# Leaving PSUM by wide ScalarE copies and normalising on GpSimd, in a top-k attention and PReLU kernel

## The chip, the cores and the metric

The kernel runs on one core of a Trainium2 chip. The time is that of one whole execution on the device, in microseconds (us). The core has engines that run side by side, each in the order of its own instruction stream: TensorE (PE; its weight loads are PEld), VectorE (DVE), ScalarE (ACT), GpSimd (POOL) and SyncE (SP), which here only starts transfers. They meet through semaphores: an instruction that needs a result waits, and everything behind it on the same engine waits too.

## The reference

Eight batches of eight heads, 576 rows of width 64. Each row of scores keeps only its 32 largest entries before the softmax; the attention output, laid out as 4608 tokens by 512, goes through two matrix products with a PReLU between them.

```python
scores = scale * np.matmul(q, k.transpose(0, 1, 3, 2))
kth = np.partition(scores, -32, axis=-1)[..., -32:-31]
scores = np.where(scores >= kth, scores, -1e9)
attn = np.exp(scores - scores.max(-1, keepdims=True))
attn = attn / (attn.sum(-1, keepdims=True) + 1e-9)
x = np.matmul(attn, v)            # then tokens x 512
h = x @ w_in
out = (np.maximum(h, 0) + alpha * np.minimum(h, 0)) @ w_out
```

## The kernel before, in words

Work goes by pairs of heads (32 pairs, four to a batch). The rows of a pair make nine row tiles of 128 x 576 scores, so there are 288 row tiles, numbered n. The program is written out by hand in **ticks**, one row tile per tick: a loop over n emits for each engine what it does in that tick, and small tables (`put`, `run`) hold work for a later tick of a given engine. Nothing reorders it afterwards.

One row tile passes the engines like this:

- PE makes the scores into PSUM (`scores`, L335). ACT copies them out with a pivot added (`act_b`, L344, tile `b`), counts how many lie on one side of the pivot (`act_s`, L349, `h`, with an accumulator read) and takes the exponential of two tiles at once (`act_e`, L354, `e`).
- POOL turns the count into a sign (`side_of`, L359, `SG`) and flips the scores by it (`flip`, L365, `y`; two buffers). In tick n it flips tile n-1.
- DVE takes the eight largest of each of five segments of `y` (L376, tile n-2 in tick n), merges those lists (L390, L392, tile n-3), and applies the resulting limit to the exponentials (`weights`, L443, tile n-7, the first DVE instruction of a tick). In one tick of three it compares counts (`sel_eq`, L408, `EQ`). For that POOL has prepared `ra` in two steps: `sel_a` (L398) in the tick before and `sel_a2` (L403) right behind the flip in the same tick. `limit` (L424, `KP`) is POOL's too.
- The weights go to a transposing transfer started by SP (L457). When those of a half pair are there, PE multiplies them with v (`av`, L495) into a PSUM tile `pu`, four or six blocks of 65 columns: 64 products and a sum of the weights. DVE takes the reciprocal of the sums (`av_rz`, tile `rz`), and `av_out` (L524, ACT) writes product times reciprocal into the row buffers `xb` (128 rows) and `xm` (64 rows), one instruction per head and chunk. SP transposes `xb` into `xT` for the two matrix products (`x_turn`, L569), whose steps fill PE and ACT between the ticks.

A pair is cut in two halves. With j the tick modulo 9, the first half (g = 0: four blocks) has `av` in a tick with j = 4, the second (g = 1: six blocks, two of them 64 rows) in one with j = 1. Pairs 0 to 26 leave PSUM through `av_out`; pair 27 does it on DVE (`dve_out`), the last batch through `out_last`, also on DVE. Neither is touched.

Of the kernel before, what the change touches and what calls it, by code (L numbers as in the profile page):

```python
# [9 lines left out]
FP32 = mybir.dt.float32  # L10
BF16 = mybir.dt.bfloat16
I32 = mybir.dt.int32
AF = mybir.ActivationFunctionType
ALU = mybir.AluOpType
# [17 lines left out]
def kernel(  # L32
# [10 lines left out]
    nc = tc.nc  # L43
    B, H, S_, D = q.shape
    NTOK, DM = out.shape
# [5 lines left out]
    KPB = H // 2  # L51
# [39 lines left out]
    prep = main.enter_context(tc.tile_pool(name="prep", bufs=2))  # L91
    attn = main.enter_context(tc.tile_pool(name="attn", bufs=4))
# [36 lines left out]
    pairs = {}  # L129
# [32 lines left out]
    n = 0  # L162
    while n < NT:
        m = 1 if ORDER[n][1] == 8 and ORDER[n + 1][1] != 8 else 2
# [291 lines left out]
            d["wT", j // 2] = wT  # L456
            nc.sync.dma_start_transpose(wT, d["w2"])  # L457

    xb, xm = {}, {}

    def check_group(g):
        nc.vector.tensor_reduce(out=M8[:, g * TPP:g * TPP + TPP], in_=Cs.pop(g)[:, :, :, 7],
# [24 lines left out]

    def x_tiles(b):
        if b not in xb:
            xb[b] = [prep.tile([128, DM], BF16, name="xb", bufs=6) for _ in range(4)]  # L490
            xm[b] = prep.tile([64, DM], BF16, name="xm", bufs=1)

    def av_one(o_, d, wT, side, cs):
# [4 lines left out]
    def av(p, g):  # L498
        d = pairs[p]
        x_tiles(p // KPB)  # L500
        d["pu", g] = pu = ps_d.tile([128, 4 + 2 * g, V1], FP32, name="pu", tag="pd")
        for i in range(2):
            for side in range(2):
                av_one(pu[:, 2 * i + side, :], d, d["wT", 2 * g + i], side, slice(0, 128))
        if g == 1:
            for side in range(2):
                av_one(pu[0:64, 4 + side, :], d, d["wTm"], side, slice(64 * side, 64 * side + 64))

    def av_rz(p, g):
        d = pairs[p]  # L510
        d["rz", g] = rz = attn.tile([128, 6], FP32, name="rz", bufs=4)
        nc.vector.reciprocal(rz[:, 0:4], d["pu", g][:, 0:4, D])
        if g == 1:
            nc.vector.reciprocal(rz[0:64, 4:6], d["pu", g][0:64, 4:6, D])

    def av_out(p, g):
        d = pairs[p]
        b, kt = p // KPB, p % KPB
        pu, rz = d["pu", g], d["rz", g]
        for c in range(4 + 2 * g):  # L520
            m = 128 if c < 4 else 64
            h0 = 128 * kt + 64 * (c % 2)
            dst = xb[b][2 * g + c // 2][:, h0:h0 + 64] if c < 4 else xm[b][:, h0:h0 + 64]
            nc.scalar.activation(dst, pu[0:m, c, 0:D], AF.Copy, scale=rz[0:m, c:c + 1])  # L524

    def dve_out(p, g):
        d = pairs[p]
        b, cs = p // KPB, slice(128 * (p % KPB), 128 * (p % KPB) + 128)
        pu, rz = d["pu", g], d["rz", g]
        for c in range(0, 4 + 2 * g, 2):  # L530
            m = 128 if c < 4 else 64
            dst = xb[b][2 * g + c // 2] if c < 4 else xm[b]
            nc.vector.tensor_tensor(
                dst[:, cs].rearrange("p (s d) -> p s d", s=2), pu[0:m, c:c + 2, 0:D],
                rz[0:m, c:c + 2].unsqueeze(2).to_broadcast([m, 2, D]), ALU.mult)
# [3 lines left out]
    def av_last(i, g):  # L539
        x_tiles(B - 1)  # L540
        m = 128 if i < 4 else 64
        pul[i, g] = pu = ps_d.tile([128, 4, V1], FP32, name="pu", tag="pd")
        for s in range(2):
            d = pairs[P0 + 2 * g + s]
            for side in range(2):
                cs = slice(0, 128) if i < 4 else slice(64 * side, 64 * side + 64)
                av_one(pu[0:m, 2 * s + side, :], d, d["wT", i] if i < 4 else d["wTm"], side, cs)

    def rz_last(i, g):
        m = 128 if i < 4 else 64  # L550
        rz = attn.tile([128, 6], FP32, name="rz", bufs=4)
        nc.vector.reciprocal(rz[0:m, 0:4], pul[i, g][0:m, :, D])
        pul[i, g] = pul[i, g], rz

    def out_last(i, g):
        m = 128 if i < 4 else 64
        pu, rz = pul.pop((i, g))
        dst = xb[B - 1][i] if i < 4 else xm[B - 1]
        nc.vector.tensor_tensor(
            dst[:, 256 * g:256 * g + 256].rearrange("p (s d) -> p s d", s=4), pu[0:m, :, 0:D],  # L560
            rz[0:m, 0:4].unsqueeze(2).to_broadcast([m, 4, D]), ALU.mult)

    def x_turn(b, chunks):
        for i in chunks:
            c0 = (b * S + 128 * i) % NX
            if b == B - 1:
                c0 = b * S % NX + (64 + 128 * i if i < 4 else 0)
            if i < 4:
                nc.sync.dma_start_transpose(xT[:, :, c0:c0 + 128], xb[b][i])  # L569
            else:  # L570
                nc.sync.dma_start_transpose(xT[:, :, c0:c0 + 64], xm[b])
# [4 lines left out]
    def turn_last(h):  # L576
        pool, tag = (ps_a, "pa") if h == 0 else (ps_m, "misc")
        xa = pool.tile([128, 2, 128], BF16, name="xa", tag=tag)
        for j in range(2):
            c0 = 128 * (2 * h + j)  # L580
            nc.tensor.transpose(xa[:, j, :], xb[B - 1][3][:, c0:c0 + 128], ident_b)
        nc.vector.tensor_copy(xT[:, 2 * h:2 * h + 2, CL:CL + 128], xa)
# [205 lines left out]
    with tc.manual_schedule(engines={E.PE, E.Activation, E.DVE, E.Pool, E.SP}):  # L788
        cal = {}

        def put(tick, eng, f):
            cal.setdefault((tick, eng), []).append(f)
# [11 lines left out]
        def feed(lim):  # L804
            while blocks and blocks[0][0] + blocks[0][1] <= lim:
                back.extend(mlp_steps(*blocks.pop(0)))
# [12 lines left out]
        def tail_of(n, wn):  # L819
            wp, wj = ORDER[wn]  # L820
            b = wp // KPB
            if wp < P0:
                if wj == 3:
                    put(n + 3, "pe", lambda: av(wp, 0))
                    put(n + 4, "dve", lambda: av_rz(wp, 0))
                    if wp == P0 - 1:
                        put(n + 4, "dvx", lambda: dve_out(wp, 0))
                    else:
                        put(n + 6, "act", lambda: av_out(wp, 0))
                    if wp % KPB == KPB - 1 and b >= 5:  # L830
                        dt = 4 if wp == P0 - 1 else 6
                        put(n + dt, "end", lambda: x_turn(b, (0, 1)))
                        put(n + dt + 2, "end", lambda: feed(b * S + 256))
                if wj == 8:
                    put(n + 4, "pe", lambda: av(wp, 1))
                    put(n + 5, "dve", lambda: av_rz(wp, 1))
                    if wp == P0 - 1:
                        put(n + 5, "dvx", lambda: dve_out(wp, 1))
                    else:
                        put(n + 7, "act", lambda: av_out(wp, 1))  # L840
                    if wp % KPB == KPB - 1:
                        dt = 5 if wp == P0 - 1 else 7
                        put(n + dt, "end", lambda: x_turn(b, range(2 if b >= 5 else 0, 5)))
                        put(n + dt + 2, "end", lambda: feed((b + 1) * S))
            elif (wj == 8 or wj % 2) and wp % 2:
                i, g = wj // 2, (wp - P0) // 2
                dt = 2
                if i == 3 and g == 1:
                    put(n + dt, "pe", flush)
                put(n + dt, "pe", lambda: av_last(i, g))  # L850
                where = "end" if i == 3 and g == 0 else "dvx"
                put(n + dt + 1, where if where == "end" else "dve", lambda: rz_last(i, g))
                put(n + dt + 1, where, lambda: out_last(i, g))
                if i == 3:
                    if g == 1:
                        put(n + dt + 1, where, lambda: last_ph(0))
                    put(n + dt + 2 - g, where, lambda: turn_last(g))
                    if g == 1:
                        put(n + dt + 1, where, lambda: (last_ph(1), last_pz()))
                elif g == 1:  # L860
                    put(n + dt + 1, "dvx", lambda: x_turn(b, (i,)))
                    put(n + dt + 2, "end", lambda: back.extend(mlp_steps(*last.pop(i))))
# [23 lines left out]
        n = 0  # L886
        end = max(NT + 24, 0)
        while n < end or back or after:
# [20 lines left out]
            if n < NT:  # L909
                n0, m, i = unit_of[n]  # L910
# [82 lines left out]
            for wn in due:  # L993
                turn(wn)
                tail_of(n, wn)
# [152 lines left out]
```

## Time and profile before

| | |
|---|---|
| three runs | 817.95, 819.47, 822.98 us (median 819.47) |
| the profiled execution | 820.06 us, of which 818.2 us span from first to last instruction |
| busy, share of the span | DVE 95%, ACT 92%, PE 86%, POOL 73% |
| mean granted TensorE clock | 0.947 of full speed |

A busy share is a mean over the whole span; how far an engine is filled in one stretch is read from the view by stretches. In the rows below, times are microseconds from the start of the span unless marked ns; what stands in brackets behind an instruction is the idle time of its engine just before it and what ended that.

### The profile page before, as it was taken

How to read it: one execution, taken by the hardware profiler on the slowest of the kernel's cores; microseconds unless marked ns; L12 is line 12 of the kernel's file. 1: busy time of each engine (PE TensorE's matmuls, PEld its weight loads, DVE VectorE, ACT ScalarE, POOL GpSimd, SP SyncE). 2: the span in 40 equal slices, each digit the busy share in tenths (PEclk: the TensorE clock that was granted, in tenths of full speed). 3: DMA queues.
4: the chain of work that ended last, by engine and by line, in shares of the span. 5: the costliest groups of instructions: out<-in, count | busy, mean ns of one | idle time of the engine just before them, and what ended most of it. 6: DMA issues, size and time to landing. Idle time of an engine off the chain costs nothing. (4 is left out here: it accounts for less than half of the span.)

```text
span 818.2 us, 20527 instructions
## 1 busy us (share of the span) xinstructions
PE 701.8 (86%) x5705; PEld 419.7 (51%) x5780; DVE 774.3 (95%) x4464; ACT 750.8 (92%) x1730; POOL 594.9 (73%) x1052
## 2 busy tenths in 40 slices
PE   7876779878978799888988789978898989999977
PEld 4533445444545446444544345644455565665755
DVE  5999999999999999999999999999999999999973
ACT  6998999999999999999999999999999999988842
POOL 5787777777777878777687777776777867676630
PEclk8587779899999999999999999999999999999999
DMA  7899985656666565565577546664556653455332
GB/s 150 170 165 174 166 141 107 122 111 97 145 140 135 98 133 122 116 123 103 124 162 123 111 97 138 121 140 96 107 127 132 121 116 87 94 108 100 84 77 59
DMA packets 343001, 99.06 MB, mean 121 GB/s; under 512 B 335056, under 2 KB 335328, under 8 KB 342880
## 3 DMA queue, kind: packets, MB, share of 16 engines
q1 hardware_dynamic: 337808, 94.73, 58.5%
q0 software_dynamic: 3584, 2.39, 2.6%
q8 instruction: 47, 0.77, 0.4%
q10 hardware_dynamic: 1488, 0.56, 0.3%
q14 instruction: 74, 0.61, 0.2%
HBM read 36.71 MB, written 9.44 MB: 56 GB/s over the span
## 5 line engine op out<-in xcount | busy, mean ns | idle before, releaser
L365 POOL TENSOR_TENSOR y<-SG,b 128x576 int32<-128x576 int32 x288 | 417.2, 1449 | 97.3 <-DVE C L376 86.7
L376 DVE MAX8 C<-y 128x8 f32<-128x112 f32 (+1 forms) x1440 | 384.0, 267 | 3.8 <-POOL y L365 3.8
L335 PE MATMUL ps<-qkT 64*128 64x288 f32 (+1 forms) x1280 | 243.8, 457 | 17.1 <-ACT b L344 16.7
L344 ACT ACTIVATE b<-ps,T 128x576 f32<-128x576 f32 x288 | 206.6, 759 | 13.6 <-PE ps L335 13.6
L443 DVE SCALAR_TENSOR_TENSOR w<-b,KP,e 128x576 bf16<-128x576 f32 x256 | 204.5, 800 | 2.3 <-POOL KP L424 2.2
L349 ACT ACTIVATE h<-b 128x576 bf16<-128x576 f32 x288 | 201.8, 701 | 2.5
L735 PE MATMUL ph<-xT,w_in_b 128*128 128x128 bf16 (+2 forms) x997 | 143.2, 285 | 50.9 <-ACT gT L741 40.4
L354 ACT ACTIVATE e<-b 128x1152 bf16<-128x1152 f32 (+1 forms) x158 | 173.7, 1099 | 0.0
L335 PEld LDWEIGHTS ps<-qkT 64*128 64x128 f32 (+1 forms) x1280 | 127.8, 187 | 79.7 <-ACT b L344 39.1
L390 DVE MAX8 L<-C 128x8 f32<-128x40 f32 x864 | 160.4, 186 | 0.2
L359 POOL TENSOR_SCALAR SG<-S_all 128x1 int32<-128x1 f32 x288 | 82.4, 286 | 96.2 <-ACT h L349 72.2
L735 PEld LDWEIGHTS <-w_in_b 128*128 128x128 bf16 x1024 | 80.2, 99 | 105.0 <-issue 80.2
L753 PE MATMUL pz<-w_out_b,gT 128*128 128x512 bf16 x544 | 132.3, 380 | 1.2 <-issue 0.3
L392 DVE MATCH_REPLACE8 C<-L,C 128x40 f32<-128x40 f32 x576 | 105.5, 183 | 0.0
L741 ACT ACTIVATE gT<-ph 128x512 bf16<-128x512 f32 x140 | 85.7, 619 | 15.2 <-PE ph L735 14.7
L753 PEld LDWEIGHTS <-gT 128*128 128x128 bf16 x560 | 51.7, 98 | 69.7 <-issue 13.2
L495 PE MATMUL pu<-v_bf,wT 128*128 128x65 bf16 (+1 forms) x1600 | 69.1, 198 | 10.4 <-DMA wT<-w 8.8
L495 PEld LDWEIGHTS <-wT 128*128 128x128 bf16 (+1 forms) x1600 | 65.1, 103 | 20.9 <-DMA wT<-w 9.3
L349 ACT ACTIVATION_READ_ACCUMULATOR h<-b 128x1 f32 x288 | 61.7, 214 | 0.0
L524 ACT ACTIVATE xb<-pu,rz 128x64 bf16<-128x64 f32 x216 | 51.9, 356 | 0.0
L392 DVE MATCH_VALUE_LOAD C<-L,C 128x8 f32 x576 | 41.6, 72 | 0.1
L758 ACT COPY o_sb<-pz 128x512 f32<-128x512 f32 x35 | 20.5, 587 | 17.8 <-PE pz L753 17.8
(117 smaller groups left out, 715.9 us busy)
## 6 DMA issues: line engine op xcount, KB each, us to landing
out_dram<-o_sb SPq DMA_DIRECT2D x34, 256.0 KB, 2.3
st_q<-in_q_dram SPq DMA_DIRECT2D x64, 128.0 KB, 2.8
kst<-in_k_dram SPq DMA_DIRECT2D x62, 128.0 KB, 2.6
st_v<-in_v_dram SPq DMA_DIRECT2D x60, 128.0 KB, 2.7
w_stage<-in_moe_w_out_dram SPq DMA_DIRECT2D x16, 256.0 KB, 4.0
w_in_b<-in_moe_w_in_dram POOLq DMA_DIRECT2D x8, 256.0 KB, 6.5
wT<-w SPq DMA_TRANSPOSE x128, 3.3
st_q<-in_q_dram SPq DMA_DIRECT2D x32, 32.0 KB, 2.6
```

The source lines that it names most:

```text
L335: nc.tensor.matmul(o_, l_, r_, start=True, stop=True)
L344: nc.scalar.activation(t["b"].rearrange("p (a c) -> p a c", a=2), t["ps"], AF.Identity, bias=T0[:, p * TPP + j:p * TPP + j + 1], scale=-ON ...
L349: nc.scalar.activation(h, tiles[n]["b"], AF.Sign, accum_out=S_all[:, n:n + 1])
L354: nc.scalar.activation(e, tiles[n0]["bu"], AF.Exp, scale=-scl)
L365: nc.gpsimd.tensor_tensor(t["y"].bitcast(I32), SG[:, n:n + 1].to_broadcast([128, S]), t["b"].bitcast(I32), ALU.subtract)
L376: return [lambda g=g: nc.vector.max(out=C[:, n % TPP, g, :], in_=y[:, g:S // 8:NSEG, :]) for g in range(NSEG)]
L390: ops.append(lambda r=r, src=src: nc.vector.max(out=L[:, 8 * r:8 * r + 8], in_=src))
L392: ops.append(lambda r=r, src=src: nc.vector.match_replace(out=C2, in_to_replace=L[:, 8 * r:8 * r + 8], in_values=src, imm_value=NEG))
L443: nc.vector.scalar_tensor_tensor(out=w_dst(n), in0=t["b"], scalar=row_limit(n), in1=t["e"], op0=ALU.is_le, op1=ALU.mult)
L495: nc.tensor.matmul(o_, wT[:, 4 * side + c, cs], d["v"][:, 5 * side + c, :], start=(c == 0), stop=(c == 4))
L735: nc.tensor.matmul(hold[f][:, i, :], w_in_b[:, kk, (f + i) * 128:(f + i + 1) * 128], xT[:, kk, c0:c0 + tb], start=(kk == 0), stop=(kk == N ...
L753: nc.tensor.matmul(pz[0:m], hold["gT"][:, f, r0:r0 + m], w_out_b[:, f, :], start=False, stop=(f == NFT - 1))
```

## The change

`av_out` is replaced by two steps. `av_copy` (ACT) copies the products out of PSUM without scaling: one instruction of 128 x 256 into a new float32 tile `ou` (one buffer), and for the second half one more of 64 x 128. `av_norm` (POOL) multiplies `ou` by the broadcast reciprocals `rz` into the row buffers, one instruction for both chunks of 128 rows, and one more for the 64 rows. For that, two chunks share one `xb` tile of 128 x 2 x 512; there are three such tiles instead of six of half the size. The ACT step stands two ticks earlier than before (at +4 and +5 in place of +6 and +7), the POOL step one tick behind it. Pair 27 and the last batch keep their DVE steps.

```diff
     def x_tiles(b):
         if b not in xb:
-            xb[b] = [prep.tile([128, DM], BF16, name="xb", bufs=6) for _ in range(4)]
+            xbt[b] = [prep.tile([128, 2, DM], BF16, name="xb", bufs=3) for _ in range(2)]
+            xb[b] = [xbt[b][i // 2][:, i % 2, :] for i in range(4)]
             xm[b] = prep.tile([64, DM], BF16, name="xm", bufs=1)
...
-    def av_out(p, g):
+    def av_copy(p, g):
         d = pairs[p]
-        b, kt = p // KPB, p % KPB
-        pu, rz = d["pu", g], d["rz", g]
-        for c in range(4 + 2 * g):
-            m = 128 if c < 4 else 64
-            h0 = 128 * kt + 64 * (c % 2)
-            dst = xb[b][2 * g + c // 2][:, h0:h0 + 64] if c < 4 else xm[b][:, h0:h0 + 64]
-            nc.scalar.activation(dst, pu[0:m, c, 0:D], AF.Copy, scale=rz[0:m, c:c + 1])
+        d["ou"] = ou = attn.tile([128, 6, D], FP32, name="ou", bufs=1)
+        nc.scalar.copy(ou[:, 0:4, :], d["pu", g][:, 0:4, 0:D])
+        if g == 1:
+            nc.scalar.copy(ou[0:64, 4:6, :], d["pu", g][0:64, 4:6, 0:D])
+
+    def av_norm(p, g):
+        d = pairs[p]
+        b, cs = p // KPB, slice(128 * (p % KPB), 128 * (p % KPB) + 128)
+        ou, rz = d["ou"], d["rz", g]
+        nc.gpsimd.tensor_tensor(
+            xbt[b][g][:, :, cs].rearrange("p c (s d) -> p c s d", s=2),
+            ou[:, 0:4, :].rearrange("p (c s) d -> p c s d", s=2),
+            rz[:, 0:4].rearrange("p (c s) -> p c s", s=2).unsqueeze(3).to_broadcast([128, 2, 2, D]),
+            ALU.mult)
+        if g == 1:
+            nc.gpsimd.tensor_tensor(
+                xm[b][:, cs].rearrange("p (s d) -> p s d", s=2), ou[0:64, 4:6, :],
+                rz[0:64, 4:6].unsqueeze(2).to_broadcast([64, 2, D]), ALU.mult)
...
-                        put(n + 6, "act", lambda: av_out(wp, 0))
+                        put(n + 4, "act", lambda: av_copy(wp, 0))
+                        put(n + 5, "pool", lambda: av_norm(wp, 0))
...
-                        put(n + 7, "act", lambda: av_out(wp, 1))
+                        put(n + 5, "act", lambda: av_copy(wp, 1))
+                        put(n + 6, "pool", lambda: av_norm(wp, 1))
```

Where the new instructions land on POOL, in the middle of the program. `L359` is `SG`, `L365` the flip; `L398`, `L403` make `ra`, `L424` makes `KP`, `L203` converts v. POOL before, two ticks with j = 3 and j = 6 and what lies between:

```order
L365 TENSOR_TENSOR y<-SG,b_6517 128x576
L398 TENSOR_SCALAR ra<-S_all 128x3
L424 TENSOR_TENSOR KP<-SG,KK 128x3
L359 TENSOR_SCALAR SG<-S_all 128x1
L365 TENSOR_TENSOR y<-SG,b_6517 128x576
L403 TENSOR_TENSOR ra<-ra 128x3
L359 TENSOR_SCALAR SG<-S_all 128x1
L365 TENSOR_TENSOR y<-SG,b_6607 128x576
L203 CAST v_bf_119<-st_v_113 128x4x64
```

POOL with the change, the same place:

```order
L365 TENSOR_TENSOR y<-SG,b_6484 128x576
L398 TENSOR_SCALAR ra<-S_all 128x3
L424 TENSOR_TENSOR KP<-SG,KK 128x3
L528 TENSOR_TENSOR xb<-ou,rz 128x2x128
L534 TENSOR_TENSOR xm<-ou,rz 64x128
L359 TENSOR_SCALAR SG<-S_all 128x1
L365 TENSOR_TENSOR y<-SG,b_6484 128x576
L403 TENSOR_TENSOR ra<-ra 128x3
L359 TENSOR_SCALAR SG<-S_all 128x1
L365 TENSOR_TENSOR y<-SG,b_6579 128x576
```

The second half's two multiplications stand between `KP` and `SG`: ahead of the sign, of the flip that needs it, and of the `ra` that follows that flip. The first half's place, three ticks on (j = 6), before:

```order
L398 TENSOR_SCALAR ra<-S_all 128x3
L424 TENSOR_TENSOR KP<-SG,KK 128x3
L451 COPY wm<-wm 128x64
L359 TENSOR_SCALAR SG<-S_all 128x1
L365 TENSOR_TENSOR y<-SG,b_6720 128x576
```

and with the change:

```order
L398 TENSOR_SCALAR ra<-S_all 128x3
L424 TENSOR_TENSOR KP<-SG,KK 128x3
L451 COPY wm<-wm 128x64
L528 TENSOR_TENSOR xb<-ou,rz 128x2x128
L359 TENSOR_SCALAR SG<-S_all 128x1
L365 TENSOR_TENSOR y<-SG,b_6688 128x576
L403 TENSOR_TENSOR ra<-ra 128x3
```

Here one multiplication has come in at the same spot, again ahead of sign, flip and `ra`. The instructions of DVE and their order are the same before and with the change.

## Rows read from the trace of the kernel before

**Rows 1.** The page: busy us, share of the span, instructions.

```profile
PE 701.8 (86%) x5705; PEld 419.7 (51%) x5780; DVE 774.3 (95%) x4464; ACT 750.8 (92%) x1730; POOL 594.9 (73%) x1052
```

**Rows 2.** By stretches: length, busy per engine with count, clock, DMA share, GB/s.

```profile
45.00:130.00 85.00, 61.20 (x419) 36.16 (x425) 82.16 (x481) 80.45 (x185) 65.30 (x115) 0.78 0.93 157
130.00:690.00 560.00, 488.35 (x3922) 282.17 (x3980) 553.43 (x3202) 540.31 (x1284) 432.08 (x754) 0.98 0.60 120
690.00:818.00 128.00, 115.66 (x1169) 80.12 (x1177) 105.01 (x574) 92.21 (x181) 66.56 (x115) 0.98 0.42 88
```

**Rows 3.** What DVE waited for from 45 to 690: total us, times, longest.

```profile
DVE P L244 <- PE pr L238: 2.3, 4, 0.8
DVE EQ L408 <- POOL ra L403: 2.1, 4, 0.7
DVE w L443 <- POOL KP L424: 0.8, 1, 0.8
DVE rz L512 <- PE pu L495: 0.6, 1, 0.6
```

**Rows 4.** Timeline of POOL around a tick with j = 3: start, us, instruction.

```profile
356.37 0.19 POOL L424 TENSOR_TENSOR KP<-SG,KK 128x3 int32<-128x3 int32 x1
356.53 0.23 POOL L359 TENSOR_SCALAR SG<-S_all 128x1 int32<-128x1 f32 x1
357.02 1.57 POOL L365 TENSOR_TENSOR y<-SG,b 128x576 int32<-128x576 int32 x1 [0.27 <-DVE C L376]
358.56 0.19 POOL L403 TENSOR_TENSOR ra<-ra 128x3 f32<-128x3 f32 x1
```

**Rows 5.** Timeline of DVE, the same stretch.

```profile
356.79 0.80 DVE L443 SCALAR_TENSOR_TENSOR w<-b,KP,e 128x576 bf16<-128x576 f32 x1
...
359.03 0.15 DVE L273 TENSOR_TENSOR sq<-M,sq 128x9 f32<-128x9 f32 x1
359.09 0.22 DVE L408 TENSOR_TENSOR EQ<-ra,iota 128x72 f32<-128x72 f32 x1
...
359.42 0.80 DVE L443 SCALAR_TENSOR_TENSOR w<-b,KP,e 128x576 bf16<-128x576 f32 x1
```

**Rows 6.** Timeline of POOL around a tick with j = 6, and DVE's two rows there.

```profile
364.15 0.23 POOL L451 COPY wm<-wm 128x64 bf16<-128x64 bf16 x1
365.54 0.23 POOL L359 TENSOR_SCALAR SG<-S_all 128x1 int32<-128x1 f32 x1 [1.16 <-DVE w L443]
365.86 1.14 POOL L365 TENSOR_TENSOR y<-SG,b 128x576 int32<-128x576 int32 x1
...
364.66 0.81 DVE L443 SCALAR_TENSOR_TENSOR w<-b,KP,e 128x576 bf16<-128x576 f32 x1
...
367.18 0.23 DVE L408 TENSOR_TENSOR EQ<-ra,iota 128x72 f32<-128x72 f32 x1 [0.25 <-POOL ra L403]
```

**Rows 7.** One line each: count, ns min/median/max of the flip and of `SG`.

```profile
L365 POOL TENSOR_TENSOR y<-SG,b x288: 1143/1571/1577, 12.4 to 788.7; 128x576 int32<-128x576 int32 x144
L359 POOL TENSOR_SCALAR SG<-S_all x288: 207/226/892, 12.0 to 788.4; 128x1 int32<-128x1 f32 x144
```

**Rows 8.** Groups by shape: busy us, mean ns of one, idle before and its releasers.

```profile
L203 POOL CAST v_bf<-st_v 128x192 bf16<-128x192 f32 x60 | 20.3, 340 | 0.0
L424 POOL TENSOR_TENSOR KP<-SG,KK 128x3 int32<-128x3 int32 x96 | 18.4, 192 | 7.7 <-DVE KK L418 7.7
L203 POOL CAST v_bf<-st_v 128x256 bf16<-128x256 f32 x30 | 11.9, 397 | 0.0
L220 ACT COPY qkT<-pt 128x128 f32<-128x128 f32 x32 | 8.3, 260 | 0.0
L618 ACT COPY o_sb<-pz 128x256 f32<-128x256 f32 x2 | 0.7, 372 | 2.8 <-SPq L1013 1.8 <-PE pz L615 1.0
L408 DVE TENSOR_TENSOR EQ<-ra,iota 128x72 f32<-128x72 f32 x96 | 21.6, 225 | 7.2 <-POOL ra L403 4.9
```

**Rows 9.** Timeline of ACT: the steps out of PSUM, second and first half.

```profile
309.36 0.94 ACT L524 ACTIVATE xb<-pu,rz 128x64 bf16<-128x64 f32 x4
310.15 0.52 ACT L524 ACTIVATE xm<-pu,rz 64x64 bf16<-64x64 f32 x2
...
317.90 0.93 ACT L524 ACTIVATE xb<-pu,rz 128x64 bf16<-128x64 f32 x4
```

More of the change, by code (lines that the diff above doesn't have):

```diff
@@ L457, in turn @@
             nc.sync.dma_start_transpose(wT, d["w2"])
-    xb, xm = {}, {}
+    xb, xm, xbt = {}, {}, {}
     def check_group(g):
```

## The prediction

> **What bounds the kernel now.** I read the page first, then the view by stretches, DVE's waits, and the timelines of POOL, DVE and ACT around the two places that the change touches. By the page DVE is the fullest engine, ACT close behind, POOL has a quarter of the span free [rows 1]. By stretches the middle is sharper: from 130 to 690 us DVE is busy 553.43 of 560 us, ACT 540.31, POOL 432.08 [rows 2]. So the middle is DVE's own work, instruction behind instruction, and DVE's instructions do not change. A cheaper ACT can give back only what DVE waits. From 45 to 690, the stretch in which the changed steps run, all its listed waits come to 2.3 + 2.1 + 0.8 + 0.6 = 5.8 us [rows 3]; the start and the end, where DVE is idle more, have no changed step of weight.
>
> One of those waits matters for its form. `EQ` waits for POOL's `ra`, and `ra` stands right behind a flip. In the tick with j = 6 the sequence shows: `SG` at 365.54, flip to 367.00, `ra` to 367.15, `EQ` at 367.18 with DVE idle for 0.25 [rows 6]. In the tick with j = 3, `ra` ends at 358.75 and `EQ` starts at 359.09, right behind DVE's previous work: a reserve of 0.34 us [rows 4, 5]. So DVE has one place per three ticks where a late flip costs it time at once. Everywhere else a flip is used a tick later.
>
> The second thing is the flip's length. It takes 1.143 us at least and 1.571 at the median [rows 7]. The short one began 1.20 us after DVE's L443 started [rows 6], the long one 0.23 after it [rows 4, 5]: POOL stands still while L443 reads its two inputs, until about 357.02 + 0.43 = 357.45, that is 0.66 after L443's start. `SG`, 0.226 at the median, has cases up to 0.892 [rows 7], so a small instruction is caught too. L443's own time stays 0.80 to 0.81 in both ticks [rows 5, 6]: POOL pays, not DVE.
>
> **What ACT saves.** The second half takes from 309.36 to 310.67 now, 1.31 us, the first 0.93 [rows 9]: 2.24 per pair. The copies: 128 x 256 out of PSUM is 0.372 (L618, the same shape), 128 columns 0.260 (L220) [rows 8]; 2 x 0.372 + 0.260 = 1.00. Saved 1.24 per pair, 33 us of ACT over 27 pairs. What covers it is DVE: of 33 us it can give the end no more than the waits above. I take 3 us: POOL waiting for ACT's `h` makes some flips, and so some `EQ`, late, and all idle time in front of `EQ` in the whole span is 7.2 us [rows 8], part of it outside 45 to 690. PSUM is freed two ticks earlier, which can only help `P` (2.3 us [rows 3]); it is within those 3. If this cover went (ACT the bound), the saving would show in full; rows 2 exclude that.
>
> **What POOL gets.** No wide float multiplication of POOL is in the trace. Nearest is the two-input integer subtraction: 0.192 us for 3 elements, 1.143 for 576 [rows 7, 8], so 1.66 ns an element beyond a fixed part. That gives 0.61 us for 256 and 0.40 for 128, 1.6 us per pair, 44 us in all; POOL's total stays under 80% of the span. The cheap end is the one-input conversion, 0.397 for 256 and, by the step from 192, 0.28 for 128 [rows 8]. The dear end is a whole flip for the 256, 1.14, and half of that for the 128. I take 0.61 and 0.40, the same operation class at another length.
>
> *Second half, j = 3.* The multiplications come between `KP` and `SG`. Take rows 4 and 5 as the clock. The first begins at 356.53; L443 starts at 356.79 and holds POOL to 357.45; 0.26 to 0.36 of its 0.61 are done by then (the hold may begin some 0.1 late), so it ends at 357.70 to 357.80. The second, overlapped by 0.03 as its neighbours are, ends at 358.07 to 358.17, `SG` at 358.27 to 358.37. The flip begins 0.09 later, as in rows 6, and is now clear of L443: it takes 1.14 and ends at 359.50 to 359.60, `ra` at 359.65 to 359.75, `EQ` starts 0.03 later, at 359.68 to 359.78. Now it starts at 359.09. DVE stands for 0.59 to 0.69, I take 0.65; behind `EQ` in DVE's order are the last segment's MAX8 and the next L443, and all that follows. 27 times: **+17.5 us**. The reserve of 0.34 and the flip's escape from the hold (0.43) are already in it. With the cheap ends the same chain has `EQ` at 359.35: +0.26, 7 us. With the dear ones about 360.38: +1.3, 35 us.
>
> By a page alone: the Trainium skill's GPSIMD Engine Reference (Performance versus the Vector engine) gives 4497 ns for 2048 elements of a two-input add, 2.2 ns each, so as an estimate 0.56 and 0.28; `EQ` would be late by about 0.42 and this term 11 us instead of 17.5.
>
> *First half, j = 6.* One multiplication begins where `wm`'s copy ends, 364.35. L443 at 364.66 cuts it; 0.31 to 0.41 is done, the rest ends by 365.62, `SG` by 365.82, against 365.77 now. In this pair `SG` was late anyway, behind ACT's `h`, so the cost is 0 to 0.05. Where `SG` was not late the `EQ` would come up to 0.3 later. I take 0.04 on average, **+1 us**.
>
> **Other edits.** The row buffers keep their bytes; the multiplication that reuses a buffer comes eight ticks after the transfers that read it were issued, some 20 us, so nothing new waits there. SP's queue: `x_turn` stays where it is, and POOL's step is one tick ahead of where ACT's was. The ACT copies come one tick behind PE's products; should PE be late, ACT waits with slack from its 1.24 us. `ou` has one buffer: a copy waits for a multiplication two ticks older. I cost these at nothing; their cover is ACT's new slack, and if it is gone, `h` is late and the flips with it, which is a rival below.
>
> **Sum.** +17.5 + 1 - 3 = +15.5 against the profiled 820.06: 835.6. The profiled execution is 0.6 over the median of the three runs, 819.47, so I say 835.
>
> **Rivals.**
>
> - *The multiplications are cheap or only partly held* (18%). Then `EQ` slips by 0.26 or less, 0 to 7 us, minus 3 on ACT's side: 817 to 824. For it: converting 256 elements takes 0.40. Against: every two-input instruction of POOL in the trace is on the other slope.
> - *Faster: ACT sets DVE's pace through `h`, `SG` and flip* (11%). If L443's hold spares the new instructions, they fit: 356.53 + 0.98 is 357.51, `SG` to 357.74, flip to 358.97, `EQ` at 359.15, no more than 0.06 late. Then ACT's relief stands alone and removes at most `EQ`'s 7.2 and `P`'s 2.3: 810 to 816. For it: the idle time at j = 6 is behind a late `SG`. Against: `SG`'s 0.892, a small instruction held. The Trainium skill (GPSIMD Engine Reference, Specifications) speaks against it too: GpSimd shares its SBUF interfaces with VectorE and contends with VectorE instructions that have two SBUF inputs, as L443 has, whatever GpSimd runs; by that rule the time is the forecast's. This decides: whether a multiplication begun just ahead of L443 runs through without costing DVE.
> - *Dearer* (8%). The multiplication with a broadcast and split rows takes about a flip's time, or a POOL instruction already under way makes L443 wait: +1.0 us and more per pair, 850 to 855.
> - *The change does not do what it says* (5%): ACT's copies wait for PE or for `ou`, so ACT keeps its old time; with DVE standing as forecast or a little less, 822 to 840.
>
> **How the numbers follow.** The forecast (58%) spans the bounds 0.35 to 0.9 per pair, 27 times, less 2: 827 to 843. The range reaches from 819, inside the cheap rival, to 849; left out are the faster one and the dear one. What a measurement of this kernel can tell from no change is about 1%, 8 us: faster is below 811.3, slower above 827.7. The forecast is slower nearly throughout (0.55 of 0.58), with the dear one 0.63 and a little of the last 0.65; the cheap rival and part of the faster one are within 1%, 0.27; faster 0.08.
>
> **What would show it.** In the new profile: ACT's busy time down by about 33 us, L524 gone, copies at 0.37; POOL up by 40 to 60; DVE's busy time as it was. `EQ` should carry a new idle time released by `ra`, about 0.65 in each tick that follows j = 3, some 15 to 20 us in all, and flips of 1.14 there in place of 1.57. It is wrong if that idle time stays under 8 us; if POOL's multiplications last under 0.45 while `SG` still starts ahead of 357.7 on rows 4's clock; or if the time falls while `EQ` waits as before, for then ACT set the pace.

## The result and the profile after

The change makes the kernel slower: 832.89 us (median of four runs, 832.39 to 834.75) against 821.09 for the kernel before in the same runs, a ratio of 1.0144 with a 95% interval of 1.0112 to 1.0176. The forecast was 835. The profiled execution took 833.21 us, 831.4 of it span.

The page of the kernel after, to be held against [rows 1]:

```profile
PE 715.8 (86%) x5780; PEld 424.7 (51%) x5780; DVE 790.7 (95%) x4464; ACT 722.0 (87%) x1541; POOL 645.3 (78%) x1133
```

ACT has 29 us less work, POOL 50 more; both were expected. What was not: DVE runs the same 4464 instructions and is busy for 16.4 us longer. The span grew by 13.2, so DVE's share stays at 95% and nothing looks different by the share alone.

The view by stretches, after (columns as in [rows 2]):

```profile
45.00:130.00 85.00, 65.09 (x427) 37.66 (x425) 84.06 (x475) 76.56 (x161) 71.08 (x125) 0.74 0.91 158
130.00:690.00 560.00, 491.26 (x3929) 282.36 (x3926) 554.74 (x3132) 507.41 (x1106) 464.50 (x804) 0.97 0.60 118
690.00:831.00 141.00, 125.67 (x1236) 84.55 (x1235) 118.24 (x650) 100.19 (x195) 79.05 (x136) 0.99 0.43 88
```

In the middle DVE is as full as before (554.74 of 560 us) but gets through 3132 instructions where it got through 3202. The work is the same, so some of its instructions have become longer; ACT meanwhile has 53 us free, 33 more than before.

Which instructions became longer is in the groups by shape. First the kernel before, lines that do not stand ahead of the prediction, then the kernel after (busy us, mean ns | idle before):

```profile
L443 DVE SCALAR_TENSOR_TENSOR w<-b,KP,e 128x576 bf16<-128x576 f32 x256 | 204.5, 800 | 2.3 <-POOL KP L424 2.2
L359 POOL TENSOR_SCALAR SG<-S_all 128x1 int32<-128x1 f32 x288 | 82.4, 286 | 96.2 <-ACT h L349 72.2 <-DVE C L376 6.4 <-ACT alpha_sb L636 5.2
L283 DVE TENSOR_TENSOR t<-sq,t 128x9 f32<-128x9 f32 x32 | 5.8, 180 | 0.1
L273 DVE TENSOR_TENSOR sq<-M,sq 128x9 f32<-128x9 f32 x32 | 4.9, 153 | 0.5 <-ACT M L269 0.5
```

```profile
L443 DVE SCALAR_TENSOR_TENSOR w<-b,KP,e 128x576 bf16<-128x576 f32 x256 | 208.5, 816 | 2.2 <-POOL KP L424 2.2
L359 POOL TENSOR_SCALAR SG<-S_all 128x1 int32<-128x1 f32 x288 | 69.1, 240 | 27.2 <-ACT h L349 11.7 <-ACT alpha_sb L648 5.2 <-DVE L L390 4.1
L528 POOL TENSOR_TENSOR xb<-ou,rz 128x256 bf16<-128x256 f32 x54 | 34.1, 631 | 0.0
L534 POOL TENSOR_TENSOR xm<-ou,rz 64x128 bf16<-64x128 f32 x27 | 23.5, 869 | 0.0
L408 DVE TENSOR_TENSOR EQ<-ra,iota 128x72 f32<-128x72 f32 x96 | 21.1, 220 | 6.8 <-POOL ra L403 6.5
L520 ACT COPY ou<-pu 128x256 f32<-128x256 f32 x54 | 20.7, 383 | 32.2 <-PE pu L496 31.4 <-POOL xm L534 0.8
L283 DVE TENSOR_TENSOR t<-sq,t 128x9 f32<-128x9 f32 x32 | 16.1, 502 | 0.1
L273 DVE TENSOR_TENSOR sq<-M,sq 128x9 f32<-128x9 f32 x32 | 9.1, 286 | 0.5 <-ACT M L269 0.5
L522 ACT COPY ou<-pu 64x128 f32<-64x128 f32 x27 | 7.0, 259 | 0.0
```

Three DVE lines carry it: L283 + 10.3 us, L273 + 4.2, L443 + 4.0, together 18.5. All three read two inputs from SBUF. L283 handles nine numbers a partition and takes 502 ns. `EQ`'s idle time, where the prediction looked for 15 to 20 us, is 6.8 and was 7.2 [rows 8]; that total hides two moves, from 0.2 to 4.5 us in the tick behind the second half's place and from 7.0 to 2.3 in all others. And a wait has gone: `SG` stood 72.2 us for ACT's `h`, now 11.7.

The second half's place: POOL and then DVE, after, the stretch that answers to [rows 4, 5]:

```profile
364.39 0.19 POOL L424 TENSOR_TENSOR KP<-SG,KK 128x3 int32<-128x3 int32 x1
364.54 0.61 POOL L528 TENSOR_TENSOR xb<-ou,rz 128x256 bf16<-128x256 f32 x1
365.11 0.91 POOL L534 TENSOR_TENSOR xm<-ou,rz 64x128 bf16<-64x128 f32 x1
366.00 0.22 POOL L359 TENSOR_SCALAR SG<-S_all 128x1 int32<-128x1 f32 x1
366.30 1.15 POOL L365 TENSOR_TENSOR y<-SG,b 128x576 int32<-128x576 int32 x1
367.40 0.20 POOL L403 TENSOR_TENSOR ra<-ra 128x3 f32<-128x3 f32 x1
```

```profile
364.82 0.95 DVE L443 SCALAR_TENSOR_TENSOR w<-b,KP,e 128x576 bf16<-128x576 f32 x1
...
367.21 0.26 DVE L273 TENSOR_TENSOR sq<-M,sq 128x9 f32<-128x9 f32 x1
367.63 0.23 DVE L408 TENSOR_TENSOR EQ<-ra,iota 128x72 f32<-128x72 f32 x1 [0.16 <-POOL ra L403]
...
367.97 0.80 DVE L443 SCALAR_TENSOR_TENSOR w<-b,KP,e 128x576 bf16<-128x576 f32 x1
```

The first multiplication is under way when L443 starts and goes through unheld, in 0.61; L443 takes 0.95 instead of 0.80. The second begins while L443 runs and is held: 0.91. The flip is late but short (1.15), and the small L273, which meets the end of it, takes 0.26. From one L443 to the next it is 3.15 us, where it was 2.63.

The first half's place, POOL and DVE, after (compare [rows 6]):

```profile
372.69 0.23 POOL L451 COPY wm<-wm 128x64 bf16<-128x64 bf16 x1
372.88 0.61 POOL L528 TENSOR_TENSOR xb<-ou,rz 128x256 bf16<-128x256 f32 x1
373.46 0.23 POOL L359 TENSOR_SCALAR SG<-S_all 128x1 int32<-128x1 f32 x1
373.86 1.57 POOL L365 TENSOR_TENSOR y<-SG,b 128x576 int32<-128x576 int32 x1 [0.17 <-DVE C L376]
```

```profile
372.82 0.15 DVE L390 MAX8 L<-C 128x8 f32<-128x40 f32 x1
372.94 0.58 DVE L283 TENSOR_TENSOR t<-sq,t 128x9 f32<-128x9 f32 x1
373.44 0.26 DVE L376 MAX8 C<-y 128x8 f32<-128x112 f32 x1
373.63 0.79 DVE L443 SCALAR_TENSOR_TENSOR w<-b,KP,e 128x576 bf16<-128x576 f32 x1
```

The multiplication runs from 372.88 to 373.49, L283 from 372.94 to 373.52: they end together. The MAX8s around it, with one input, keep their times (0.15 and 0.26). So do all 1440 of L376 in this run, 247 to 286 ns, though 1041 of them start while a POOL instruction is under way.

Summed over ticks 18 to 250, taken from start to start of L443 (`w` and `wm`), the time goes from 622.1 to 635.6 us: stretches of the second half's place have a median of 3154 ns instead of 2632 (+0.52 a pair, 14 us in all over 27 pairs), those of the first half's place 3047 instead of 2630 (+0.42 or 11), and four other ticks of each nine (j = 0, 1, 5, 7) together give about 0.4 a pair, 10 to 11 us, back.

### The profile page after: what moved, and what is told of

It reads as the page before. It is cut to its first block, busy times and chain, and to the rows that moved or that the text cites. A ratio compares the mean times of both kernels' runs of the same rounds, so it can differ in the third digit from the quotient of the medians.

```text
span 831.4 us, 20465 instructions
## 1 busy us (share of the span) xinstructions
PE 715.8 (86%) x5780; PEld 424.7 (51%) x5780; DVE 790.7 (95%) x4464; ACT 722.0 (87%) x1541; POOL 645.3 (78%) x1133
## 4 chain that ended last, share of the span: by engine, by line
DVE 58%; POOL 17%; PE 13%; ACT 5%; issue 4%; DMA 1%; SPq 1%; POOLq 0%; ACTq 0%; DVEq 0%
DVE C L376 19%; DVE w L443 14%; POOL y L365 9%; DVE C L392 8%; DVE L L390 7%; PE pz L765 3%; PE ps L335 3%; PE ph L747 3%; POOL xm L534 3%; DVE P L244 2%; DVE L L414 2%; DVE wm L443 2%; DVE EQ L408 2%; PE pu L496 1%; ACT b L344 1%
## 5 line engine op out<-in xcount | busy, mean ns | idle before, releaser
L365 POOL TENSOR_TENSOR y<-SG,b 128x576 int32<-128x576 int32 x288 | 429.2, 1490 | 127.5 <-DVE C L376 120.6
L376 DVE MAX8 C<-y 128x8 f32<-128x112 f32 (+1 forms) x1440 | 381.5, 265 | 3.8 <-POOL y L365 3.8
L443 DVE SCALAR_TENSOR_TENSOR w<-b,KP,e 128x576 bf16<-128x576 f32 x256 | 208.5, 816 | 2.2 <-POOL KP L424 2.2
L747 PE MATMUL ph<-xT,w_in_b 128*128 128x128 bf16 (+2 forms) x1024 | 147.8, 290 | 37.3 <-ACT gT L753 24.5
L335 PEld LDWEIGHTS ps<-qkT 64*128 64x128 f32 (+1 forms) x1280 | 129.7, 188 | 75.7 <-ACT b L344 35.9
L496 PE MATMUL pu<-v_bf,wT 128*128 128x65 bf16 (+1 forms) x1600 | 72.3, 203 | 32.7 <-DVE P L244 22.8
L496 PEld LDWEIGHTS <-wT 128*128 128x128 bf16 (+1 forms) x1600 | 68.4, 106 | 47.4 <-issue 32.7
L359 POOL TENSOR_SCALAR SG<-S_all 128x1 int32<-128x1 f32 x288 | 69.1, 240 | 27.2 <-ACT h L349 11.7
L765 PEld LDWEIGHTS <-gT 128*128 128x128 bf16 x560 | 51.7, 98 | 69.7 <-issue 13.2
L349 ACT ACTIVATION_READ_ACCUMULATOR h<-b 128x1 f32 x288 | 59.5, 207 | 0.0
L520 ACT COPY ou<-pu 128x256 f32<-128x256 f32 x54 | 20.7, 383 | 32.2 <-PE pu L496 31.4
```

The lines of the kernel that those rows point to most:

```text
L335: nc.tensor.matmul(o_, l_, r_, start=True, stop=True)
L349: nc.scalar.activation(h, tiles[n]["b"], AF.Sign, accum_out=S_all[:, n:n + 1])
L365: nc.gpsimd.tensor_tensor(t["y"].bitcast(I32), SG[:, n:n + 1].to_broadcast([128, S]), t["b"].bitcast(I32), ALU.subtract)
L376: return [lambda g=g: nc.vector.max(out=C[:, n % TPP, g, :], in_=y[:, g:S // 8:NSEG, :]) for g in range(NSEG)]
L443: nc.vector.scalar_tensor_tensor(out=w_dst(n), in0=t["b"], scalar=row_limit(n), in1=t["e"], op0=ALU.is_le, op1=ALU.mult)
L496: nc.tensor.matmul(o_, wT[:, 4 * side + c, cs], d["v"][:, 5 * side + c, :], start=(c == 0), stop=(c == 4))
```

## The experiments

Times are medians; each ratio is against the kernel before in the same runs. The diffs are against the kernel after. What each theory expected was on record before its run. My theory A, from the profile above: a GpSimd multiplication makes DVE's instructions with two SBUF inputs wait, and ACT's relief is worth some 10 us by itself.

**Copies alone.** ACT's wide copies write the row buffers directly; the division by the sums is left out.

```diff
-        nc.scalar.copy(ou[:, 0:4, :], d["pu", g][:, 0:4, 0:D])
+        nc.scalar.copy(xbt[b][g][:, :, cs].rearrange("p c (s d) -> p c s d", s=2),
+                       d["pu", g][:, 0:4, 0:D].rearrange("p (c s) d -> p c s d", s=2))
...
-                        put(n + 5, "pool", lambda: av_norm(wp, 0))
...
-                        put(n + 6, "pool", lambda: av_norm(wp, 1))
```

> Leaves out the division by the sum of the weights: ScalarE's wide copies write the row buffers directly and GpSimd gets no multiplication, so the rows stay unnormalised. Theory A (each GpSimd multiplication stands in VectorE's way at its place, 0.54 us per pair in the second half and 0.40 in the first, 24 us in all, while ScalarE's relief gives about 10 us back): 808 to 812 us. Rival B (as forecast: ScalarE's relief is worth no more than 3 us, and the loss is smaller than it looks): 817 to 820.

811.87 us, 0.9882 (0.9851 to 0.9913): A. ACT's relief gives 9.5 us, so POOL's multiplications cost 21. DVE is busy 769.8 us, L283 takes 181 ns and L443 799, `EQ`'s idle time is 4.4.

**One half at a time.** The old `av_out` for the second half (diff), then for the first.

```diff
-                        put(n + 5, "act", lambda: av_copy(wp, 1))
-                        put(n + 6, "pool", lambda: av_norm(wp, 1))
+                        put(n + 7, "act", lambda: av_out(wp, 1))
```

First half new:

> Only the first half of a pair goes the new way (one multiplication per pair); the second half leaves PSUM by the old ScalarE step. Theory A: +10 from VectorE's two-input instruction L283 waiting while the multiplication runs, minus 4 to 5 of ScalarE's relief: 825 to 828, with L283 at about 0.58 us in the ticks with j = 6. Rival B (the loss sits in the second half, where a flip is late for EQ): 818 to 822.

818.1 us, 0.9958 (0.9937 to 0.9979). Its number is B's, but B's reason does not hold: the loss is in place, L283 at 502 ns as in the full change:

```profile
L283 DVE TENSOR_TENSOR t<-sq,t 128x9 f32<-128x9 f32 x32 | 16.1, 502 | 0.1
```

A had halved the relief along with the change; one half gives nearly all of it.

Second half new:

> Only the second half goes the new way (two multiplications per pair); the first half leaves PSUM by the old ScalarE step. Theory A: +14 minus about 6 of ScalarE's relief: 827 to 831. Rival B: all of the loss, with little relief: 833 to 837.

825.1 us, 1.0045 (1.0025 to 1.0065), just below A's range. L443 is at 814 ns, L273 at 286, `EQ` idle 8.6, L283 back at 180. Singly the halves move the time by -3.3 and +3.7, together by +11.8: each alone gets nearly the whole relief, which both together get once. By these times, with 9.5 of relief, the first half costs some 6 us and the second 13; the stretches above gave 11 and 14, and that difference stays open.

**One input instead of two on POOL.** Plain copies of GpSimd in place of the multiplications; the division is left out here too.

```diff
-        nc.gpsimd.tensor_tensor(
+        nc.gpsimd.tensor_copy(
             xbt[b][g][:, :, cs].rearrange("p c (s d) -> p c s d", s=2),
-            ou[:, 0:4, :].rearrange("p (c s) d -> p c s d", s=2),
-            rz[:, 0:4].rearrange("p (c s) -> p c s", s=2).unsqueeze(3).to_broadcast([128, 2, 2, D]),
-            ALU.mult)
+            ou[:, 0:4, :].rearrange("p (c s) d -> p c s d", s=2))
```

> Leaves out the division: GpSimd copies ou into the row buffers, one input instead of two, at the same places. Theory A1 (a GpSimd instruction under way keeps VectorE's two-input instructions waiting whatever its own inputs): L283 near 0.36 us, 0.2 less than with the change because the copy takes 0.40 instead of 0.61; the time 822 to 827. Rival A2 (only two-input GpSimd instructions do that): L283 at 0.18, no L443 over 0.82, and 814 to 820.

820.34 us, 0.9984 (0.9964 to 1.0005). The lines, first the copy and then L283:

```profile
L528 POOL CAST xb<-ou 128x256 bf16<-128x256 f32 x54 | 22.6, 418 | 0.0
L283 DVE TENSOR_TENSOR t<-sq,t 128x9 f32<-128x9 f32 x32 | 10.3, 322 | 0.1
```

A1's mechanism: the copy is 0.2 us shorter than the multiplication, and so is L283. DVE's L283 waits for what POOL has under way, with one input or two. The time lies between the two ranges.

**Moved.** The multiplications one tick later, behind `ra` in place of ahead of `SG`; the copies go one tick later too, and the 64 rows get a tile and a tick of their own.

```diff
-                        put(n + 5, "pool", lambda: av_norm(wp, 0))
+                        put(n + 6, "pool", lambda: av_norm(wp, 0))
...
-                        put(n + 6, "pool", lambda: av_norm(wp, 1))
+                        put(n + 7, "pool", lambda: av_norm(wp, 1))
+                        put(n + 8, "pool", lambda: av_norm_m(wp))
```

> All three multiplications as in the change, but one tick later, behind the ra step, where VectorE runs only one-input instructions: first half in the tick with j = 7, second half with j = 4, its 64 rows with j = 5 in a tile of their own; the copies one tick later too. Theory A (only the place costs): near the kernel without multiplications, 809 to 815 us, L283 back at 0.18 and no long L443. Rival C (GpSimd's load costs, wherever it stands: 50 us more busy on an engine that must flip one tile per tick): 828 to 834 as with the change.

825.76 us, 1.006 (1.0042 to 1.0078): both missed. L283 (182 ns) and L443 (798) are free, but three others now meet the multiplications. `EQ` itself has two inputs; L276, a TENSOR_SCALAR on nine int32 numbers, has only one:

```profile
L408 DVE TENSOR_TENSOR EQ<-ra,iota 128x72 f32<-128x72 f32 x96 | 28.0, 291 | 3.3 <-POOL ra L403 2.8
L273 DVE TENSOR_TENSOR sq<-M,sq 128x9 f32<-128x9 f32 x32 | 9.1, 283 | 0.5 <-ACT M L269 0.5
L276 DVE TENSOR_SCALAR t<-sq 128x9 int32<-128x9 int32 x32 | 10.5, 329 | 0.1
```

Against the run with copies alone, `EQ` is 6.9 us longer in all, L276 5.2 (it took 166 ns there) and L273 4.3, together 16.4; the time is 13.9 longer. Most of the L276s start under the 64-row multiplication and end about 30 ns behind it. So two SBUF inputs are not the whole condition.

**L283 earlier.** The change, with L280 and L283 one tick ahead of POOL's multiplication.

```diff
         if p > 1:
+            ts[10] = ts[11] = -4
+            steps[10] = {dvx: [dve_4]}
```

> The change, with VectorE's reciprocal L280 and the two-input step L283 behind it done one tick earlier, so that L283 no longer meets the first half's multiplication. Theory A (any VectorE instruction with two inputs in SBUF waits while a GpSimd instruction is under way): the wait passes partly to L443, the next such instruction, which would start 0.2 us before the multiplication ends; 3 to 7 us are won, 826 to 830. Rival D (L283 is long for a reason of its own, such as its operand from L280): it stays at 0.5 us and the time at 832 to 834.

839.48 us, 1.0219 (1.0193 to 1.0245): neither. L283 is at 174 ns, but the collision has only moved. POOL, then DVE at the first half's place (lines have shifted by three: L446 is the old L443):

```profile
377.19 0.61 POOL L531 TENSOR_TENSOR xb<-ou,rz 128x256 bf16<-128x256 f32 x1
377.76 0.74 POOL L362 TENSOR_SCALAR SG<-S_all 128x1 int32<-128x1 f32 x1
378.58 1.15 POOL L368 TENSOR_TENSOR y<-SG,b 128x576 int32<-128x576 int32 x1
...
377.29 1.12 DVE L446 SCALAR_TENSOR_TENSOR w<-b,KP,e 128x576 bf16<-128x576 f32 x1
```

Without L283 ahead of it the large L446 is there in time to meet the multiplication and waits 0.32; `SG`, begun under it, is held (0.74), so the flip is late. L283's wait had been shielding L446. The `L280` and `L283` moved also lengthen the tick they went to (median 2.62 to 3.04 us).

**First half, tuned.** Only the first half new, its multiplication ahead of the copy of `wm`, L283 earlier.

```diff
-                        put(n + 5, "pool", lambda: av_norm(wp, 0))
+                        put(n + 5, "pool0", lambda: av_norm(wp, 0))
...
+            run(n, "pool0")
```

> Only the first half goes the new way, its multiplication stands ahead of wm's copy (0.2 us earlier), and L280 and L283 are one tick earlier; the second half as before the change. Theory A: the multiplication now ends about when L443 begins, so the cost of 10 us at j = 6 falls to 0 to 4: 808 to 814. Rival D: as with the first half alone, 817 to 820.

826.5 us, 1.0068 (1.0046 to 1.0089): both wrong. The multiplication now meets the start of L446, and the `wm` copy behind it is held under L446:

```profile
369.51 0.61 POOL L531 TENSOR_TENSOR xb<-ou,rz 128x256 bf16<-128x256 f32 x1
370.06 0.76 POOL L454 COPY wm<-wm 128x64 bf16<-128x64 bf16 x1
370.80 0.23 POOL L362 TENSOR_SCALAR SG<-S_all 128x1 int32<-128x1 f32 x1
371.11 1.15 POOL L368 TENSOR_TENSOR y<-SG,b 128x576 int32<-128x576 int32 x1
```

L446 takes 0.95 there, and `EQ` comes late.

**Both halves, tuned.** The same, with the second half new in three pairs of four, its copies in bfloat16 and its multiplications in the next period.

```diff
+                    elif wp % KPB == KPB - 1:
+                        put(n + 7, "act", lambda: av_out(wp, 1))
...
-                        put(n + 6, "pool", lambda: av_norm(wp, 1))
+                        put(n + 12, "pool", lambda: av_norm(wp, 1))
+                        put(n + 12, "pool", lambda: av_norm_m(wp))
```

> As first_tuned, and in three of four pairs the second half goes the new way too, with its multiplications in the next tick with j = 0, the longest one (3.13 us), which has no EQ; its copies in bfloat16 for room. Theory A: ScalarE's full relief at little cost, near the kernel without multiplications: 808 to 815. Rival C (GpSimd's load itself costs): 820 or more.

833.01 us, 1.0147 (1.0122 to 1.0172): C's side. The loss of the first half is there again, L446 at 817 ns, and `EQ`'s idle time is 14.3 us.

**Spread.** The next theory: what counts is which DVE instruction stands beside the multiplication. In a tick with j = 2 POOL has a conversion of v (L203, [rows 8]) behind the flip, beside MAX8s and reciprocals of DVE. The first half's multiplication takes that place, the conversion goes to j = 0, the second half stays old, and so does one pair of the first.

```diff
+            ts[13:] = [t - 2 * ((BASE[p] + t) % 9 == 2) for t in ts[13:]]
...
-                        put(n + 5, "pool", lambda: av_norm(wp, 0))
+                        put(n + 10, "pool", lambda: av_norm(wp, 0))
...
-                        put(n + 5, "act", lambda: av_copy(wp, 1))
-                        put(n + 6, "pool", lambda: av_norm(wp, 1))
+                        put(n + 7, "act", lambda: av_out(wp, 1))
```

> Only the first half goes the new way, and its multiplication waits until the next tick with j = 2: there it follows the flip in place of a conversion of v (0.34 us), which goes to j = 0, the longest tick; no EQ and no wm copy stands in that tick, and VectorE's next two-input instructions there, L414 and L443, come about 2.3 and 2.67 us after the tick's first L443, the multiplication from 1.8 to 2.4. Pair 23 keeps the old step. Theory A (only what meets a two-input VectorE instruction or delays a flip that an EQ needs costs time): the 10 us of the first half fall to 0 to 2: 807 to 812. Rival C (any 0.6 us on GpSimd costs): 817 to 820, as with the first half alone.

811.66 us, 0.9871 (0.9845 to 0.9897): A, and the fastest complete version of the kernel here. POOL, then DVE around it (L444 is the old L443):

```profile
352.00 1.57 POOL L366 TENSOR_TENSOR y<-SG,b 128x576 int32<-128x576 int32 x1 [0.50 <-DVE C L377]
353.54 0.61 POOL L529 TENSOR_TENSOR xb<-ou,rz 128x256 bf16<-128x256 f32 x1
354.12 0.21 POOL L360 TENSOR_SCALAR SG<-S_all 128x1 int32<-128x1 f32 x1
...
351.77 0.80 DVE L444 SCALAR_TENSOR_TENSOR w<-b,KP,e 128x576 bf16<-128x576 f32 x1
354.11 0.27 DVE L415 TENSOR_TENSOR L<-EQ,L 128x72 f32<-128x72 f32 x1
354.49 0.80 DVE L444 SCALAR_TENSOR_TENSOR w<-b,KP,e 128x576 bf16<-128x576 f32 x1
```

Only the last 0.04 us of the multiplication meets a two-input instruction. L283 is at 180 ns, L444 at 800.

**Spread, both halves.** The second half too, in j = 5 and j = 0, in three pairs of four; v is converted in two steps, and `ou` has one buffer for both halves.

```diff
+            t8 = next(t for t in range(-10, -1) if (BASE[p] + t) % 9 == 8)
+            ts[13:] = [t8, t8 + 1]
...
+                        put(n + 6, "act", lambda: av_copy(wp, 1))
+                        put(n + 8, "pool", lambda: av_norm(wp, 1))
+                        put(n + 12, "pool", lambda: av_norm_m(wp))
```

> Both halves the new way: the first at j = 2 as in spread_first, the second half's 128 rows at j = 5, its 64 rows at j = 0; v is converted in two instructions instead of three (j = 8 and j = 0); every fourth pair keeps the old step for the second half. Theory A: three places with 0.05 to 0.1 us of overlap each, 5 us in all, against a little more relief on ScalarE: 809 to 816. Rival C: 825 to 833.

831.9 us, 1.0114 (1.0086 to 1.0141): A missed, and the time is in C's range. The waits from 45 to 700 us name another cause than load:

```profile
ACT ou L522 <- POOL xb L531: 36.2, 24, 2.3
DVE rz L515 <- ACT ou L522: 16.0, 20, 1.1
```

The second half's copy waits until the first half's multiplication has read `ou`; the reciprocal on DVE waits behind that copy. L283 (172 ns) and L445 (801) are clean. So the same with a tile for each half, the second half's in bfloat16, and its copy at +5:

```diff
-        d["ou"] = ou = attn.tile([128, 4, D], FP32, name="ou", bufs=1)
+        d["ou", g] = ou = attn.tile([128, 4, D], BF16 if g else FP32, name=f"ou{g}", bufs=1)
```

> As spread_both, but each half has its own copy tile (the second half's in bfloat16 for room), so that a ScalarE copy no longer waits for the other half's multiplication one tick behind it, and VectorE's reciprocal no longer waits for that copy. Theory A (spread_both was lost to that buffer, not to the multiplications): 808 to 816. Rival C (three multiplications per pair cost by their load): 825 to 832 again.

813.25 us, 0.9904 (0.9864 to 0.9944): A. POOL is busy 631.1 us, 36 more than before and close to the change's 645.3, and the kernel is faster by 1%, within noise of the run with copies alone (0.9882), with 68 of the change's 81 multiplications. So it is the place of the multiplications that costs, not POOL's load.

## Why the prediction was right, and where it was not

- **The bound** held: DVE's own stream sets the middle, before and after.
- **The prices** held. The multiplication of 256 takes 0.61 us unheld, that of 64 rows 0.39 (its mean where moved; 0.40 was taken); ACT's copies 383 and 259 ns (372 and 260), ACT 29 us lighter (33), POOL 50 busier (40 to 60). The Trainium skill's GPSIMD Engine Reference (Performance versus the Vector engine) had led to an estimate of 0.56 and 0.28; these rows decide for the longer ones. (By that estimate the prediction's chain gives an `EQ` late by 0.42 to 0.52, so 11 to 14 us; it took the lower end.)
- **The second half** was to cost 0.65 a pair and cost 0.52, 14 us against 17.5, composed differently. The step that failed is "POOL pays, not DVE", drawn from flips that begin under L443 [rows 4, 5]. No row of before showed the reverse order at that place, a long POOL instruction already under way when L443 starts. Elsewhere the trace of before did show it, in L276 (the rows below this list). With the change, DVE waits at the second half's place: 0.15 in L443, 0.11 in L273 (in the pair shown). And the multiplication that was to be held part way goes through. Of the other 0.26, 0.16 is `EQ`'s idle time, and about 0.09 is the overlap of L273 and `EQ`, lost in that wait.
- **The first half** was to cost 0.04 a pair and cost 0.42, about 11 us against 1. The same step failed: I followed `SG` and `EQ`, not DVE's small L283.
- **ACT's relief** was taken at 3 us and is 9.5 alone, by the run with copies only. I counted only the idle time in front of DVE's instructions. DVE also became 4.5 us less busy there, `EQ`'s idle time fell by 2.8 and that in front of `P` by 2.5. Of the 4.5, 1.5 is L276, no longer held as often. How the relief splits beyond that stays open. It is nearly all there with one half new.
- So the sum came out near by luck, by errors that offset each other: + 18.5 - 3 forecast, about + 25 - 11 read from the stretches, + 11.8 measured (+ 13.2 between the two profiled spans).
- **The sign that would show it wrong** did appear: `EQ`'s idle time stays under 8 us, and DVE's busy time, forecast as it was, rose by 16.4. The late flip exists, 4.5 us of idle time where 15 to 20 were expected, but as a mechanism it is the smaller part. Of the rivals, the dear one had the right form (an instruction under way makes DVE wait), at a price of 0.94 a pair for both places, but without the relief (its own 850 to 855 needs 1.2 a pair, not 1.0). The faster one named the right question, and the answer is that the multiplication does run through, at DVE's cost.
- **The other edits** cost nothing, as said; the single `ou` held ACT for 0.8 us. It became a cost only when the multiplications were moved apart.

The reverse order in the kernel before: L276, 166 ns at the median, begins under a flip and takes 0.79 us, to 0.04 behind the flip's end.

```profile
700.82 1.14 POOL L365 TENSOR_TENSOR y<-SG,b 128x576 int32<-128x576 int32 x1
701.21 0.79 DVE L276 TENSOR_SCALAR t<-sq 128x9 int32<-128x9 int32 x1
```

What the Trainium skill states (GPSIMD Engine Reference, Specifications), that GpSimd contends with VectorE instructions of two SBUF inputs or in a 2-port perf mode, agrees with these traces for two inputs: L283 takes 502 ns beside the multiplication and 180 without it. That row does not say which engine waits, so, other than the prediction says, it does not lead to the forecast's time by itself; that the one that comes later waits, on either side, the runs show. L276 waits with one SBUF input; whether it runs in such a mode no trace here shows.

## What to carry to other kernels

Before giving GpSimd work beside a full VectorE, list VectorE's instructions with two SBUF inputs, small ones too, and those with one that vary in length from one time to the next, as L276 does. Put the work beside the others, here MAX8s: the multiplications cost 21 us in one place, and most of them next to nothing in another (813.25 us against 811.87 with copies alone). Look for such waits in the mean duration of an instruction against its kernel before, because a busy share and the list of waits do not show them. Removing one collision lets the next instruction into its place, so follow both engines' order one step further before moving anything.

## What the runs showed of the hardware

- The hold between VectorE and GpSimd works both ways: POOL's `SG` under the old L443 took 0.74 instead of 0.23 (L283 earlier), the 64-row multiplication 0.91 instead of 0.39; L443 met by a multiplication took 0.95 (the change) or 1.12 (L283 earlier) instead of 0.80, and an instruction on nine numbers 0.58 instead of 0.18.
- The wait is inside the instruction's duration and counts as busy: DVE 774.3 to 790.7 us with the same instructions.
- A one-input copy on GpSimd (418 ns) does it too: L283 takes 322 ns beside it, 180 before.
- One input on VectorE's side is no safe mark. The MAX8s of L376 are not touched (at most 286 ns in 1440), but L276, a TENSOR_SCALAR on int32, is: 329 ns on average where moved, 166 with copies alone.
